# Attention feeding a two-layer MLP on one core: layer 2 of the third batch's last group in seven block products, and the attention of the last two chunks moved together

## The chip, the cores and the metric

One Trainium2 chip, one of its cores. The metric is the device time of one execution in microseconds (us), the median of several runs.

## What is computed

Two stages, in float32. Attention over 4 batches, 8 heads, 768 positions and a head size of 64: each query sees the keys within 16 positions and 24 summaries of 32 keys each (maximum of the keys, mean of the values). Its output, 3072 rows of 512, goes through a two-layer MLP.

```python
def _attn_ref(q, k, v):
    ...
    k_sum = k.reshape(B, H, nb, block, D).max(axis=3)
    v_sum = v.reshape(B, H, nb, block, D).mean(axis=3)
    scores_l = scale * np.matmul(q, k.transpose(0, 1, 3, 2))          # kept where |i - j| < 16
    scores_s = scale * np.einsum('bhsd,bhnd->bhsn', q, k_sum) + np.log(block)
    ...                                                               # softmax over both together
    return np.matmul(a, v_all)

def _moe_ref(x, w_in, w_out):      # x 3072 x 512, w_in 512 x 2048, w_out 2048 x 512
    h = x @ w_in
    g = np.maximum(0.01 * h, h)
    return g @ w_out
```

## The kernel before, in words

**Precision.** Every MLP operand is kept as two parts, hi and lo, and a product of two operands is three TensorE (PE) matmuls: hi by hi, lo by hi, hi by lo. A part is made by ScalarE (ACT; the hi part, a rounded copy) and VectorE (DVE; the lo part, the difference), so each new operand costs one instruction on each of the two.

**Stages.** The work runs in batches 0 to 3 of 768 rows, each of two chunks of 384. Batch 0 uses the plain product in both layers (`mlp`, lines 724 and 743 to 745). Batches 1 to 3 (`strassen`) take layer 1 as seven block products in place of eight, in Strassen's manner. The 16 feature tiles of 128 are taken in groups of four (n = 0 to 3), two pairs j of tiles in each. For a pair, the seven products (line 1090, names "1" to "7" in the order 1, 6, 7, 5, 2, 4, 3) go to four PSUM buffers, X (1, 2), Y (6), W (7, 4) and Z (5, 3). VectorE combines them (`add`, line 1126: U2, U3, P1), ScalarE and VectorE apply the activation and split the result (lines 1138 to 1152). Each product needs one half of the batch's input, made by `convert` (sums of the four quarters, line 955; their parts, lines 963 and 964), and a sum of weights, loaded from HBM into a ring of slots (line 1108).

**Layer 2, two ways.** In batches 1 and 2 a group's layer 2 is the plain one: six blocks of output (two halves h, three row tiles i), each of 12 matmuls of 512 columns (line 1229, tiles named L), and VectorE adds each finished block to the output row tile (line 1251, names y and rows). In batch 3 it is `second`: seven block products for each of three row tiles, each of 6 matmuls of 256 columns (line 1040, tiles named B2 or B, in the order 1, 4, 5, 7, 6, 2, 3). Its operands are G, the four activated quarters and the three differences and sums of them (`total`, line 1170, with parts at 1173 and 1177), and sums of output weights, made once for each pair j by `prepare2` (lines 865 to 877) and loaded again at line 1022. VectorE adds each product to its part of the output (`flush`, lines 1049 to 1053), named U, D, C21, C11 and C12; when the last group's product "6" is there, `merge` (line 1014) adds U into C21 and C12 and C21 into D. Two products share each PSUM half-buffer (4 and 7 in W, 5 and 3 in Z), so the later one waits until VectorE has read the earlier.

**Order.** `Plan.order` lays out the instructions of all engines by a list schedule: each operation has a due time (`prio`), and an engine takes the ready one that is due first. Due times come from a table and some numbers at the head of the file: `PLACE` for the attention of each chunk (in units of 1/24 of a batch's time), `P2` for `prepare2`, `PG` for the layer 1 weight sums, `CV` for the conversion of batch 1, `AHEAD` for how early weights are loaded. The attention of chunks 2 to 7 is spread in bursts between the MLP's matmuls (scores at line 371, transposes at 388, values at 394). Each engine then runs its list in order, and waits where an operand is not there yet.

**Buffers.** `settle` deals out slots. The ring of batch 3, `ring3`, has six slots in the input weights' place and six in output weights that are no longer read; batches 1 and 2 have `ring`, eight slots. Temporaries of batch 3 (`tmp3`) have five buffers and six pieces of `big`.

The change and the prediction touch `second` (lines 990 to 1070), `strassen` (1072 to 1259), `convert` (933 to 977) and `prepare2` (860 to 880).

Of the kernel before, what the change touches and what calls it, by code (L numbers as in the profile page):

```python
# [13 lines left out]
ALU = mybir.AluOpType  # L14
# [10 lines left out]
TPC = 3  # L25
T = 128 * TPC
# [10 lines left out]
SPL = 10  # L37
FP = 4
PARTS = [(0, 0, SPL), (1, 0, NF), (0, SPL, NF), (2, 0, FP), (3, 0, FP)]
CV = 26.64187  # L40
PG = 2.38096
P2 = 56.037475
XB = (0, 1, 1, 0)
SB = 2
PLACE = {0: (0.0, 1.0), 1: (13.07, 0.61), 2: (24.128751, 0.979249), 3: (33.570341, 0.464868), 4: (39.468202, 0.605071), 5: (53.449962, 0.361478), 6: (58.988368, 0.872963), 7: (67.160878, 1.199752)}
PLACE.update({c: (59.84 + UPC * (c - 6), 1.0) for c in range(8, NCH)})
LATE = 23.650498
RS = 8
GF = 4
L1W = 0.327846  # L50
AHEAD = 2.529455
BACC = {"dynamic_dma_scratch_size": 1024}

PL = -1.175
# [5 lines left out]
KP = -1.757  # L60
KS = -4
XW = 1
B1 = 2.589473
B2 = 2.761653
USQ = 1.589009
WT = 1.15
W0 = -1.523
WO = 1.029
# [95 lines left out]
def DVE(n, fast=False):  # L164
    return 65 + (0.52 if fast else 1.042) * n
# [6 lines left out]
def build(tc, ctx, a):  # L172
# [816 lines left out]

    def second(b, n, tn, g_op, done, rows):  # L990
        js, last = (2 * n, 2 * n + 1), n == NF // GF - 1
        letter = {"1": "X", "2": "X", "4": "W", "7": "W", "5": "Z", "3": "Z", "6": "Y"}
        goal = {"1": "U", "6": "U", "4": "D", "5": "D", "7": "C21", "2": "C11", "3": "C12"}
        part = {"D": (0, 256), "C21": (0, 0), "C11": (1, 0), "C12": (1, 256)}
# [8 lines left out]
        def keys(name, i):  # L1003
            return ("U", b, i) if name == "U" else ("y", b, part[name][0], i)
# [7 lines left out]

        def merge(x, y, i, t, after):
            return P.op("DVE", DVE(256), t, lambda: nc.vector.tensor_tensor(out=acc(x, i), in0=acc(x, i), in1=acc(y, i), op=ALU.add), after=after, use=[keys(x, i), keys(y, i)])

        for pos, q in enumerate(ORDER2):
            t = tn + L1W + pos * (6 - L1W) / 7
# [6 lines left out]
            for i in range(TPC):  # L1024
                tag, x = HALF2[s][i]
                kb = ("B2", b, n, tag)
                fresh = kb not in opened

                def block(q=q, i=i, tag=tag, x=x, kb=kb, fresh=fresh):
                    o = bank(kb, tag) if fresh else tl[kb]  # L1030
                    m = 0
                    for j in js:
                        gh, gl = (y[:, 128 * i:128 * i + 128] for y in g_of2(j, q))
                        if q in MEM2:
                            w = [ring(("r2", b, j, q))[:, l] for l in range(2)]
# [10 lines left out]
                def flush(name=name, q=q, i=i, kb=kb, x=x):  # L1046
                    y, z = acc(name, i), tl[kb][:, x:x + 256]
                    if n == 0 and q in "1723":
                        nc.scalar.copy(y, z)
                    elif n == 0 and q == "4":  # L1050
# [5 lines left out]
                e = ("ACT", ACT(256, True)) if n == 0 and q in "1723" else ("DVE", DVE(256))  # L1056
                p = P.op(e[0], e[1], t + 0.01 * i - 1.0, flush, after=[o] + done.get((name, i), []), use=[kb] + ([] if al else [k]), alloc=al)
                half[s, i] = [o, p]
                done[name, i] = [p]
                if not last:  # L1060
                    continue
                if q == "6":
                    for y in ("C21", "C12"):
                        done[y, i] = [merge(y, "U", i, t + 0.01 * i - 0.9, done[y, i] + [p])]
                    done["D", i] = [merge("D", "C21", i, t + 0.01 * i - 0.85, done["D", i] + done["C21", i])]
                if q in "63":
                    h = int(q == "3")
                    ky = ("y", b, h, i)
                    P.op("SP", 550, t + 0.5, lambda c=CPB * b + h, i=i, ky=ky: nc.sync.dma_start(out=a["out"][c * T + 128 * i:c * T + 128 * i + 128, :], in_=tl[ky]),
                         after=done["C11", i] + [p] if h else done["D", i], use=[ky], size=128 * 2048)  # L1070

    def strassen(b, t0):
        done, two = {}, b == B - 1
        n0 = FP // GF if b == 1 else 0
        if b == 1:
            done = {(h, i): [spill_op[2 + h, i]] for h in range(2) for i in range(TPC)}
# [16 lines left out]
            return P.op("PE", 6 * (T / 2.4 + 14.5), t, run, after=after + conv_op[b, pos], use=[kr, kx] + ([] if start else [kb]), alloc=[(tag, kb, 1)] if start else [])  # L1093

        for n in range(n0, NF // GF):
            tn = t0 + 6 * n
            g_op = {}
            for j in (2 * n, 2 * n + 1):
                K = lambda s, j=j: (s, b, j)
# [5 lines left out]
                for pos, q in enumerate(ORDER):  # L1105
# [6 lines left out]
                    p_op[q] = o = product(j, q, kr, kx, tags[s], (K(s), start), t, [lr] + hold.get(s, []), [])  # L1112
                    d = t - 1.0
                    def tmp(key):
                        if P.slot[key][0] != "q":
                            return new(P.slot[key], key, [128, T], bufs=1)
                        n = int(P.slot[key][1:])
                        tl[key] = raw[:, T * n:T * n + T]
                        return tl[key]
                    pool3 = "tmp3" if two else "tmp"  # L1120
                    ps = lambda s, K=K: tl[K(s)][:, :T]

                    def add(out, s, y, first, prio, after, K=K, ps=ps):
# [163 lines left out]
        t += UPC * (f1 - f0) / NF  # L1287
    for j in range(NF // 2):
        prepare(j, LEAD + 13 + PG * j)
        prepare2(j, LEAD + P2 + 3.5 * j)  # L1290
    for b in range(1, B):
        convert(b, LEAD + (24 * b - 3.2 if b > 1 else CV))
        strassen(b, LEAD + 24 * b)
# [1 line left out]
    P.settle("h", lambda t: ("h0", "h1"))  # L1295
    P.settle("big", lambda t: [f"big{n}" for n in range(BIG if t < LATE else 3)])
    P.settle("tmp", lambda t: ("gs", "ghi0", "glo0", "ghi1", "glo1"))
    P.settle("tmp3", lambda t: ["gs", "ghi0", "glo0", "ghi1", "glo1"] + [f"q{n}" for n in range(6)])
    P.settle("ring", lambda t: [f"r{n}" for n in range(RS)])
    P.settle("ring3", lambda t: [f"r{n}" for n in (0, 1, 2, 3, 6, 7)] + [f"b{n}" for n in range(6)])  # L1300
# [22 lines left out]
        begin(f"b{n}", region2[f] + region2[f + 2])  # L1323
    for i in range(TPC):
        begin(f"U{i}", early(0))
    for n in range(6):
        begin(f"q{n}", [o for p in {T * n // 512, (T * n + T - 1) // 512} for o in P.users["R", B - 1, p]])

# [68 lines left out]
```

## Time and profile before

| | |
|---|---|
| median of 3 runs | 613.03 us (612.43 to 613.39) |
| the profiled execution, its own time | 612.7 us |
| its span, first to last instruction | 610.9 us |
| TensorE busy | 604.9 us (99%), 4676 matmul records |
| VectorE busy | 469.7 us (77%) |
| ScalarE busy | 351.1 us (57%) |
| granted TensorE clock | 1.00 throughout |

A busy share counts the time in which at least one instruction of the engine is running. Matmuls overlap, so a busy TensorE is not yet one at its peak: the time of a stretch of matmuls is read from start to start. The groups of batches 2 and 3 lie at these times (us from the span's start): batch 2, last group, 453.13 to 485.94; batch 3, groups 0 to 3, from 485.94, 516.37, 546.51 and 576.65 to the end at 610.9.

### The profile page before, as it was taken

What the parts mean: (1) busy time and instruction counts of PE and PEld (TensorE: products, weight loads), DVE (VectorE), ACT (ScalarE), POOL (GpSimd) and SP (SyncE); (2) the same over time, 40 slices, a digit from 0 to 9 for tenths busy, and PEclk for the clock granted to TensorE, in tenths of its full rate; (3) what the DMA queues carried; (4) which work ended last, traced back from release to release, by engine and by line L of the source; (5) the groups of instructions that cost most, each with busy time, mean ns of one, the idle gap of its engine ahead of it and who ended that gap; (6) DMA issues with size and microseconds to landing.
All of it is one profiled execution on the core that took longest, in us unless ns stands there. A gap on an engine that the chain in (4) does not pass through costs nothing.

```text
span 610.9 us, 12895 instructions
## 1 busy us (share of the span) xinstructions
PE 604.9 (99%) x4676; PEld 540.1 (88%) x4676; DVE 469.7 (77%) x1281; ACT 351.1 (57%) x965; POOL 4.4 (1%) x10
## 2 busy tenths in 40 slices
PE   9999999999999999999999999999999999999997
PEld 6688889889888889999898897989889899999996
DVE  5899999953989995536688875877987783868687
ACT  5899996553776676416466665753717262606060
POOL 0200000000000000000000000000000000000000
PEclk9999999999999999999999999999999999999999
DMA  8898998896878826526497563866757484757552
GB/s 298 245 282 273 288 301 245 269 325 198 288 240 244 252 64 197 167 65 190 120 292 229 175 219 120 280 202 216 257 183 231 143 236 143 237 152 229 156 155 103
DMA packets 82926, 129.99 MB, mean 213 GB/s; under 512 B 7024, under 2 KB 50608, under 8 KB 82864
## 3 DMA queue, kind: packets, MB, share of 16 engines
q1 hardware_dynamic: 82864, 129.18, 68.1%
q8 instruction: 37, 0.61, 0.4%
q14 instruction: 25, 0.20, 0.1%
HBM read 97.72 MB, written 29.36 MB: 208 GB/s over the span
## 4 chain that ended last, share of the span: by engine, by line
PE 91%; DVE 4%; ACT 2%; DMA 1%; issue 0%; SPq 0%; DVEq 0%
PE L L1229 19%; PE h L724 12%; PE X L1090 8%; PE W L1090 8%; PE Z L1090 7%; PE B_a L1040 5%; PE a L744 4%; PE a L745 4%; PE a L743 4%; PE Y L1090 4%; PE B_s L1040 2%; PE B_to L1040 1%; ACT e L383 1%; PE vps L284 1%; DMA big<-in_k_dram 1%; DVE big L687 1%
## 5 line engine op out<-in xcount | busy, mean ns | idle before, releaser
L724 PE MATMUL h<-x,win_hi 128*128 128x384 f32 x320 | 82.7, 339 | 0.0
L383 ACT ACTIVATE e<-e,m 128x120 f32<-128x120 f32 x192 | 73.7, 388 | 3.7 <-DVE m L376 3.5
L1229 PE MATMUL L<-wout_hi,win_hi 128*128 128x512 f32 x168 | 66.5, 396 | 0.0
L1229 PE MATMUL L<-wout_hi,win_lo 128*128 128x512 f32 x168 | 65.7, 391 | 0.0
L1229 PE MATMUL L<-wout_lo,win_hi 128*128 128x512 f32 x168 | 65.6, 391 | 0.0
L724 PEld LDWEIGHTS h<-x,win_hi 128*128 128x128 f32 x320 | 57.6, 188 | 2.3 <-issue 0.2
L724 PE MATMUL h<-x,win_lo 128*128 128x384 f32 x160 | 53.8, 336 | 0.0
L743 PE MATMUL a<-wout_hi,ghi 128*128 128x512 f32 x120 | 48.4, 403 | 0.0
L745 PE MATMUL a<-wout_hi,glo 128*128 128x512 f32 x120 | 47.3, 394 | 0.0
L744 PE MATMUL a<-wout_lo,ghi 128*128 128x512 f32 x120 | 47.1, 392 | 0.1
L1229 PEld LDWEIGHTS L<-wout_hi,win_lo 128*128 128x128 f32 x168 | 31.5, 188 | 6.8
L383 ACT ACTIVATION_READ_ACCUMULATOR e<-e,m 128x1 f32 x192 | 36.7, 191 | 0.0
L1229 PEld LDWEIGHTS L<-wout_lo,win_hi 128*128 128x128 f32 x168 | 31.6, 188 | 5.7
L1229 PEld LDWEIGHTS L<-wout_hi,win_hi 128*128 128x128 f32 x168 | 31.6, 188 | 5.7
L734 DVE TENSOR_TENSOR glo<-gs,ghi 128x384 fp32r<-128x384 f32 x40 | 22.1, 554 | 17.0 <-ACT gs L728 16.3
L731 ACT ACTIVATE ghi<-h 128x384 fp32r<-128x384 f32 x40 | 19.6, 490 | 25.9 <-PE h L724 25.9
L1186 ACT COPY P<-X 128x384 f32<-128x384 f32 x19 | 9.0, 473 | 37.0 <-PE X L1090 36.9
L724 PEld LDWEIGHTS h<-x,win_lo 128*128 128x128 f32 x160 | 30.0, 188 | 0.0
L745 PEld LDWEIGHTS a<-wout_hi,glo 128*128 128x128 f32 x120 | 22.5, 188 | 5.4 <-DVE glo L734 0.4
L315 ACT COPY k<-big 128x288 f32<-128x288 f32 x64 | 24.8, 434 | 4.1 <-DMA big<-in_k_dram 4.0
L744 PEld LDWEIGHTS a<-wout_lo,ghi 128*128 128x128 f32 x120 | 22.6, 188 | 3.9 <-DVE wout_lo L693 0.4
L743 PEld LDWEIGHTS a<-wout_hi,ghi 128*128 128x128 f32 x120 | 22.6, 188 | 3.3
(620 smaller groups left out, 1625.9 us busy)
## 6 DMA issues: line engine op xcount, KB each, us to landing
win_hi<-sums SPq DMA_DIRECT2D x73, 256.0 KB
win_lo<-sums SPq DMA_DIRECT2D x71, 256.0 KB
big<-in_w_dram SPq DMA_DIRECT2D x32, 512.0 KB
sums<-big SPq DMA_DIRECT2D x32, 512.0 KB
v<-in_v_dram SPq DMA_DIRECT2D x32, 288.0 KB
big<-in_k_dram SPq DMA_DIRECT2D x16, 400.0 KB
k<-in_q_dram SPq DMA_DIRECT2D x32, 192.0 KB
wout_hi<-sums SPq DMA_DIRECT2D x21, 256.0 KB
```

The lines of the kernel that those rows point to most:

```text
L315: nc.scalar.copy(k, x)
L383: nc.scalar.activation(out=e[:, n], in_=e[:, n], func=AF.Exp, scale=-1.0, bias=m[:, n:n + 1], accum_out=z[:, n:n + 1])
L724: nc.tensor.matmul(h[:, :T], w[:, 512 * f + 128 * k:512 * f + 128 * k + 128], x[:, T * k:T * k + T], start=n == 0, stop=n == 11)
L731: nc.scalar.activation(out=gnew(tag, G("ghi", f)), in_=tl[G("h", f)][:, :T], func=AF.Prelu, alpha=0.01)
L734: nc.vector.tensor_tensor(out=gnew(tag, G("glo", f)), in0=tl[G("gs", f)], in1=tl[G("ghi", f)].bitcast(F32), op=ALU.subtract)
L743: nc.tensor.matmul(o, gh, wout_hi[:, f], start=f == f0, stop=False)
L744: nc.tensor.matmul(o, gh, wout_lo[:, f], start=False, stop=False)
L745: nc.tensor.matmul(o, gl, wout_hi[:, f], start=False, stop=f == f1 - 1)
L1040: nc.tensor.matmul(o[:, x:x + 256], g, w[l], start=fresh and m == 0, stop=m == 5, skip_group_check=True)
L1090: nc.tensor.matmul(o[:, :T], w[:, l, 128 * k:128 * k + 128], x[y][:, T * k:T * k + T], start=start and n == 0, stop=n == 5, skip_group_che ...
L1186: nc.scalar.copy(tmp(K("P1")), ps("X"))
L1229: nc.tensor.matmul(o, g, w[:, f], start=s + m == 0, stop=s == 1 and m == 5)
```

## The change

In batch 2 the last group (n = 3, feature tiles 12 to 15) takes its layer 2 from `second` as well. Since the output of batch 2 holds plain sums by then, `second` opens with one subtraction for each row tile (D becomes D - C21), product "1" starts U afresh by a ScalarE copy, and the merges end the batch. The group takes its loads from `ring3` and its temporaries from a new list, `tmp2`, with five pieces of `big` that K and V loads and `prepare2` used until then. The pairs 6 and 7 come first in `prepare2`. The table and the numbers of the order are new: the attention of chunks 2 to 7 has other places (chunk 5 starts at 47.91 in place of 53.45, chunk 7 takes 0.88 units for a tile in place of 1.20), and layer 1 has some 0.40 units in a group where it had 0.33.

```diff
-P2 = 56.037475
+N2 = 3
+P2 = 52.764603
-PLACE = {... 5: (53.449962, 0.361478), 6: (58.988368, 0.872963), 7: (67.160878, 1.199752)}
+PLACE = {... 5: (47.912053, 0.177619), 6: (59.244554, 0.831721), 7: (69.466097, 0.878535)}
-L1W = 0.327846
-AHEAD = 2.529455
+L1W = 0.399817
+AHEAD = 2.650579
...
     def second(b, n, tn, g_op, done, rows):
+        joins = b < B - 1 and n == N2
+        opens = b == B - 1 and n == 0
...
+        if joins:
+            for i in range(TPC):
+                rows.update(("y", b, h, i) for h in range(2))
+                for name in part:
+                    done[name, i] = done[part[name][0], i]
+                done["D", i] = done["C21", i] = [P.op("DVE", DVE(256), tn + 0.1 * i, lambda i=i: nc.vector.tensor_tensor(out=acc("D", i), in0=acc("D", i), in1=acc("C21", i), op=ALU.subtract),
+                                                      after=done["D", i], use=[keys("D", i)])]
...
+                copies = opens and q in "1723" or joins and q == "1"
...
-        done, two = {}, b == B - 1
+        done = {}
...
-            tn = t0 + 6 * n
+            tn, two = t0 + 6 * n, b == B - 1 or b == B - 2 and n >= N2
...
-                    pool3 = "tmp3" if two else "tmp"
+                    pool3 = ("tmp3" if b == B - 1 else "tmp2") if two else "tmp"
...
-        prepare2(j, LEAD + P2 + 3.5 * j)
+        prepare2(j, LEAD + P2 + 3.5 * ((j - 2 * N2) % (NF // 2)))
...
+    P.settle("tmp2", lambda t: ["gs", "ghi0", "glo0", "ghi1", "glo1"] + [f"m{n}" for n in range(5)])
...
+    for n in range(5):
+        begin(f"m{n}", early(1) + early(2))
```

**How the instructions move, on VectorE**, between the end of batch 2 and the first sums of batch 3 (line 1251 adds a plain block, 1066 is the flush of `second`, 1017 its merge, 955/956 and 964/965 are the conversion of batch 3's input, U2 and U3 the first sums of batch 3). Before:

```order
L964 TENSOR_TENSOR x0_80<-big_87,x0_80 128x768
L1251 TENSOR_TENSOR y_2_0_2_4688<-L_2_3_0_2_5775,y_2_0_2_4688 128x512
L955 TENSOR_TENSOR big_87<-big_87 128x768
L1251 TENSOR_TENSOR rows_3243<-L_2_3_1_0_5786,rows_3243 128x512
L964 TENSOR_TENSOR win_lo_74<-big_87,win_hi_73 128x768 x2
L1251 TENSOR_TENSOR rows_3243<-L_2_3_1_1_5812,rows_3243 128x512
L1251 TENSOR_TENSOR rows_3243<-L_2_3_1_2_5823,rows_3243 128x512
L1126 TENSOR_TENSOR U2_3_0_5873<-Y_3_0_5856,P1_3_0_5863 128x384
```

And now:

```order
L1066 TENSOR_TENSOR rows_3243<-rows_3243,B2_2_3_to_5747 128x256 x2
L1066 TENSOR_TENSOR rows_3243<-rows_3243,B2_2_3_s0_5757 128x256
L965 TENSOR_TENSOR win_lo_74<-big_87,win_hi_73 128x768
L965 TENSOR_TENSOR x3_86<-big_87,x1_82 128x768
L956 TENSOR_TENSOR big_87<-big_87 128x768
L1066 TENSOR_TENSOR rows_3243<-rows_3243,B2_2_3_a1_5808 128x256
L956 TENSOR_TENSOR big_87<-big_87 128x768
L1066 TENSOR_TENSOR rows_3243<-rows_3243,B2_2_3_a1_5808 128x256
L1066 TENSOR_TENSOR rows_3243<-rows_3243,B2_2_3_a2_5790 128x256
L965 TENSOR_TENSOR win_lo_74<-big_87,win_hi_73 128x768 x2
L965 TENSOR_TENSOR x0_80<-big_87,x0_80 128x768
L1139 TENSOR_TENSOR U2_3_0_6013<-Y_3_0_5953,P1_3_0_5961 128x384
```

Before, the conversion was over when the last blocks were added. Now seven of its eleven instructions stand among and behind the last flushes, and the three flushes of the last product (buffers a1 and a2) stand behind two of its sums.

**On TensorE**, the first products of batch 3 (the first matmul of each product is shown; X_3_0 is product buffer X of batch 3, pair 0, and W writes PSUM bank a1). Before:

```order
L1090 MATMUL X_3_0_5847<-x1_82,win_hi_73 128x384
...
L1090 MATMUL Y_3_0_5856<-win_hi_73 128x384
...
L1090 MATMUL W_3_0_5866<-win_hi_73,win_lo_74 128x384
...
L1090 MATMUL Z_3_0_5876<-win_hi_73,win_lo_74 128x384
...
L1090 MATMUL X_3_1_5915<-x1_82,wout_hi_75 128x384
```

And now:

```order
L1103 MATMUL X_3_0_5945<-x1_82,wout_lo_76 128x384
...
L1103 MATMUL Y_3_0_5953<-win_hi_73,wout_lo_76 128x384
...
L1103 MATMUL X_3_0_5945<-x1_82,win_lo_74 128x384
...
L1103 MATMUL W_3_0_5984<-win_hi_73 128x384
...
L1103 MATMUL X_3_1_5994<-x1_82,win_lo_74 128x384
...
L1103 MATMUL Z_3_0_6003<-win_hi_73 128x384
```

Product "2" of pair 0 (the second X) now stands ahead of the first W, and product "1" of pair 1 ahead of the first Z.

## Rows read from the trace of the kernel before

**Rows 1.** The page's head: the span, and of each engine the busy time, its share and the instructions.

```profile
span 610.9 us, 12895 instructions
PE 604.9 (99%) x4676; PEld 540.1 (88%) x4676; DVE 469.7 (77%) x1281; ACT 351.1 (57%) x965; POOL 4.4 (1%) x10
```

**Rows 2.** Busy time by stretch: a busy stretch of batches 1 and 2, the last two groups of batch 2, and the four groups of batch 3. Columns: stretch, its length, busy us of PE, PEld (weight loads), DVE, ACT and POOL with the instructions, granted clock, share of the DMA engines, GB/s.

```profile
303.03:344.94 41.91, 41.91 (x379) 36.71 (x379) 35.02 (x96) 27.38 (x80) 0.00 (x0) 1.00 0.78 233
417.44:453.13 35.69, 35.69 (x235) 31.79 (x235) 30.70 (x69) 17.44 (x41) 0.00 (x0) 1.00 0.70 239
453.13:485.94 32.81, 32.81 (x193) 29.49 (x193) 25.68 (x40) 16.35 (x28) 0.00 (x0) 1.00 0.54 171
485.94:516.37 30.43, 29.95 (x212) 29.73 (x211) 19.63 (x42) 14.19 (x35) 0.00 (x0) 1.00 0.72 214
516.37:546.51 30.14, 30.14 (x212) 29.75 (x211) 22.66 (x52) 11.28 (x25) 0.00 (x0) 1.00 0.63 193
546.51:576.65 30.14, 30.14 (x211) 29.76 (x211) 23.12 (x54) 10.91 (x24) 0.00 (x0) 1.00 0.62 193
576.65:610.90 34.25, 30.16 (x210) 29.56 (x209) 26.26 (x64) 10.91 (x24) 0.00 (x0) 1.00 0.38 123
```

**Rows 3.** The chain of work that ended last, in order of time: start us, length us, engine, tile, line, instructions. A whole plain group (72), one product of layer 1 (6), a burst of attention values, a run of 36 matmuls of `second`.

```profile
252.13 16.36 PE L L1229 x72
...
471.00 1.08 PE s_('B', 24)_5734 L394 x32
...
485.94 1.06 PE X L1090 x6
487.00 1.06 PE Y L1090 x6
...
533.25 4.30 PE B_a L1040 x36
```

**Rows 4.** TensorE's timeline where layer 2 begins in group 1 of batch 3: start us, length, line, operation.

```profile
529.93 1.03 PE L1090 MATMUL Z<-x,wout_lo 128*128 128x384 f32 x5
530.79 0.28 PE L1040 MATMUL B_to<-wout_hi,win_hi 128*128 128x256 f32 x1
```

**Rows 5.** All waits of TensorE over 0.2 us from 230 us on, and its weight loads' from 440 us on: us in total, times, longest.

```profile
PE B_a L1040 <- DVE y L1051: 0.5, 1, 0.5
...
PEld B_a L1040 <- DVE y L1051: 0.7, 1, 0.7
PEld B_s L1040 <- DVE big L1053: 0.5, 3, 0.2
```

**Rows 6.** VectorE's timeline where it is never idle: two additions of 512 and a pair of 768 (batch 2), the sums of 384 (batch 3, last group), and flushes and merges of 256. The pace is the distance of the starts.

```profile
475.18 0.68 DVE L1251 TENSOR_TENSOR y<-L,y 128x512 f32<-128x512 f32 x1
475.78 1.82 DVE L964 TENSOR_TENSOR win_lo<-big,win_hi 128x768 fp32r<-128x768 f32 x2
477.51 0.95 DVE L955 TENSOR_TENSOR big<-big 128x768 f32<-128x768 f32 x1
...
584.72 0.55 DVE L1170 TENSOR_TENSOR S<-big 128x384 f32<-128x384 f32 x1
585.30 0.56 DVE L1170 TENSOR_TENSOR big<-big,C 128x384 f32<-128x384 f32 x1
585.89 0.56 DVE L1170 TENSOR_TENSOR big<-big 128x384 f32<-128x384 f32 x1
...
586.84 0.55 DVE L1177 TENSOR_TENSOR win_lo<-big,win_hi 128x384 fp32r<-128x384 f32 x1
587.30 0.55 DVE L1126 TENSOR_TENSOR U<-W,U 128x384 f32<-128x384 f32 x1
587.77 0.55 DVE L1177 TENSOR_TENSOR win_lo<-S,win_hi 128x384 fp32r<-128x384 f32 x1
...
601.69 0.42 DVE L1014 TENSOR_TENSOR rows<-rows,big 128x256 f32<-128x256 f32 x1
602.03 0.41 DVE L1053 TENSOR_TENSOR big<-big,B_s 128x256 f32<-128x256 f32 x1
602.36 0.42 DVE L1014 TENSOR_TENSOR y<-y 128x256 f32<-128x256 f32 x1
```

**Rows 7.** VectorE's timeline from batch 2 to batch 3; in brackets the idle time before, and what ended it.

```profile
481.32 1.82 DVE L964 TENSOR_TENSOR win_lo<-big,win_hi 128x768 fp32r<-128x768 f32 x2
484.62 0.69 DVE L1251 TENSOR_TENSOR rows<-L,rows 128x512 f32<-128x512 f32 x1 [1.49 <-PE L L1229]
485.98 0.69 DVE L1251 TENSOR_TENSOR rows<-L,rows 128x512 f32<-128x512 f32 x1 [0.67 <-PE L L1229]
488.17 0.56 DVE L1126 TENSOR_TENSOR U<-Y,P 128x384 f32<-128x384 f32 x1 [1.50 <-PE Y L1090]
```

**Rows 8.** ScalarE's casts of 768 and 384 from 440 us on: busy us, mean ns, idle before.

```profile
L1173 ACT CAST win_hi<-big 128x384 fp32r<-128x384 f32 x9 | 4.4, 511 | 0.0
L963 ACT CAST win_hi<-big 128x768 fp32r<-128x768 f32 x4 | 3.3, 835 | 4.7 <-DVE big L955 4.7
```

More of the change, by code (lines that the diff above doesn't have):

```diff
@@ L39 @@
 PARTS = [(0, 0, SPL), (1, 0, NF), (0, SPL, NF), (2, 0, FP), (3, 0, FP)]
-CV = 26.64187
-PG = 2.38096
-P2 = 56.037475
+N2 = 3
+CV = 27.697487
+PG = 1.958344
+P2 = 52.764603
 XB = (0, 1, 1, 0)
 SB = 2
-PLACE = {0: (0.0, 1.0), 1: (13.07, 0.61), 2: (24.128751, 0.979249), 3: (33.570341, 0.464868), 4: (39.468202, 0.605071), 5: (53.449962, 0.361478), 6: (58.988368, 0.872963), 7: (67.160878, 1.199752)}
+PLACE = {0: (0.0, 1.0), 1: (13.07, 0.61), 2: (24.128751, 0.975826), 3: (33.609766, 0.479768), 4: (40.098663, 0.520481), 5: (47.912053, 0.177619), 6: (59.244554, 0.831721), 7: (69.466097, 0.878535)}
 PLACE.update({c: (59.84 + UPC * (c - 6), 1.0) for c in range(8, NCH)})
@@ L62 @@
 XW = 1
-B1 = 2.589473
-B2 = 2.761653
-USQ = 1.589009
+B1 = 2.648168
+B2 = 2.651731
+USQ = 0.165218
 WT = 1.15
@@ L1044, in second, with flush @@
                 opened.setdefault(kb, [o])
-                def flush(name=name, q=q, i=i, kb=kb, x=x):
+                copies = opens and q in "1723" or joins and q == "1"
+                def flush(name=name, q=q, i=i, kb=kb, x=x, copies=copies):
                     y, z = acc(name, i), tl[kb][:, x:x + 256]
-                    if n == 0 and q in "1723":
+                    if copies:
                         nc.scalar.copy(y, z)
-                    elif n == 0 and q == "4":
+                    elif opens and q == "4":
                         nc.vector.tensor_scalar(out=y, in0=z, scalar1=-1.0, scalar2=None, op0=ALU.mult)
@@ L1055, in second @@
                 k = keys(name, i)
-                e = ("ACT", ACT(256, True)) if n == 0 and q in "1723" else ("DVE", DVE(256))
+                e = ("ACT", ACT(256, True)) if copies else ("DVE", DVE(256))
                 p = P.op(e[0], e[1], t + 0.01 * i - 1.0, flush, after=[o] + done.get((name, i), []), use=[kb] + ([] if al else [k]), alloc=al)
@@ L1114, in tmp @@
                     def tmp(key):
-                        if P.slot[key][0] != "q":
+                        if P.slot[key][0] not in "qm":
                             return new(P.slot[key], key, [128, T], bufs=1)
-                        n = int(P.slot[key][1:])
-                        tl[key] = raw[:, T * n:T * n + T]
+                        x = T * int(P.slot[key][1:]) + (3072 if P.slot[key][0] == "q" else 1024)
+                        tl[key] = big[:, x:x + T]
                         return tl[key]
-                    pool3 = "tmp3" if two else "tmp"
+                    pool3 = ("tmp3" if b == B - 1 else "tmp2") if two else "tmp"
                     ps = lambda s, K=K: tl[K(s)][:, :T]
```

## The prediction, made before the run

> **What bounds the kernel now.** I read the page's head first: TensorE is busy in 604.9 of 610.9 us [rows 1]. A busy TensorE may still stand in a wait, so I looked at its waits next: from 230 us on there is one over 0.2 us, in the first group of batch 3, 0.5 us before a product whose half-buffer VectorE had not yet read [rows 5]. The clock is 1.00 in every stretch, and VectorE and ScalarE have idle time in each of them [rows 2]. So TensorE's own matmuls set the time where the change lies. What is worth something is fewer or shorter matmuls, as long as the other engines still hand over their operands in time. The chain gives the price of a stretch of matmuls: here its pieces are TensorE's, one behind the other [rows 3].
>
> **Part 1, the matmuls exchanged.** The group loses 72 matmuls of 512 columns and gets 7 x 3 x 6 = 126 of 256. The 72 took 16.36 us [rows 3], 0.227 each. 36 of the others took 4.30 us [rows 3], 0.119 each, so 126 take 15.05 with no wait among them: **-1.3 us**. Layer 1 keeps its 84 matmuls: in group 1 of batch 3 they start with the group at 516.37 [rows 2], and layer 2 begins at 530.79 [rows 4], so 14.4 us. That group needs 30.14 us in all [rows 2], which leaves 15.7 for its layer 2: 0.7 us of it waits, among them those of [rows 5]. I count such waits in part 2, from 15.05.
>
> **Part 2, the work on VectorE.** Between its first sum of the group and its first sum of batch 3, VectorE had 18 instructions of 384 columns, 11 of 768 (the conversion), 6 of 512, and one each of 1024 and 256. Now it has 32 of 384, 11 of 768 and 27 of 256 (18 flushes, 9 merges). Back to back they start 0.47 (384), 0.33 (256), 0.87 (768) and 0.60 us (512) apart [rows 6]. Before: 8.4 + 9.5 + 3.6 + some 1.5 = 23 us, in a group of 32.8 [rows 2], and it stood idle 1.5, 0.7 and 1.5 us around the group's end [rows 7]. Now: 14.9 + 9.5 + 9.0 = 33.4 us, in a group where TensorE needs 14.4 + 15.05 and 1.3 for one burst of attention values (1.08 [rows 3] with its ends), 30.8 us. VectorE has more work than the group lasts, and it falls behind.
>
> Whom does that hold up? In the last group of batch 3 VectorE's first difference (tile S) starts at 584.72, 8.1 us after the group's start at 576.65 [rows 2, 6], with the same seven instructions ahead of it. From there I go by the new order: up to the flush that releases PSUM bank a1 stand 25 instructions of 384, 8 of 768 and 26 of 256, so 11.7 + 6.9 + 8.7 = 27.3 us. Three waits add some 0.75: two differences that need the one before start 0.58 apart, not 0.47 [rows 6], 0.1 each; a cast for gx has to stand behind two casts of 768 on ScalarE, 0.84 each [rows 8], some 0.4; the last W product 0.1. The flush is then over 36.2 us after the group's start, and seen by TensorE a little later, 36.3. TensorE is done with the group at 30.8 and can do X, Y and X of batch 3 meanwhile, 1.04 each [rows 3], so it stands at W at 33.9. The product W writes a1 and must wait: **+2.4 us** of waits up to here, those inside layer 2 among them. Its bounds: 0, if the order lets VectorE start its dense stretch earlier than the pattern of batch 3 (where it starts 8.1 us after the group), and 3.4, if the casts on ScalarE cost another microsecond.
>
> Queued behind W on TensorE are all other products. Behind the late flush on VectorE stand three more instructions of the conversion and the first sums of batch 3, so product Z ("5"), which reads one of these, can wait again for 0.3 us, and the second pair's W for 0.5.
>
> **Part 3, the first group of batch 3.** It took 30.43 us [rows 2], of which 14.4 + 15.05 are matmuls: 1.0 us of waits. The new order runs both X products of a pair early, and layer 2 begins between the last products of layer 1, with two blocks of product "2" ahead of "5", so that the wait on the half-buffer [rows 5] should go. Against that stand the two waits after W. I take 0.4 in place of 1.0, **-0.6 us**; bounds -1.0 and +0.3.
>
> **At nothing.** The attention makes the same matmuls, in as many bursts after 233 us (21 entries from other matmuls in either order), so its place costs TensorE nothing; its work on VectorE and ScalarE falls into groups with idle time: 30.70 of 35.69 us busy in the group before, and no wait of TensorE even where VectorE had 35.02 of 41.91 [rows 2, 5]. `prepare2`, all of it ahead of the group now, is covered by the same. If that cover were gone, its last two or three pairs would come on top of part 2. The three subtractions that open `second` lie in the group before, 1 us of VectorE's idle time. ScalarE gets 9 instructions more in all and was busy for 16.35 of 32.81 us [rows 2]. SP's queue carries eight more loads of 256 KB: 171 GB/s become some 240, and 239 and 233 ran without a wait of TensorE [rows 2, 5]. The six stores of batch 2 now wait on SP for the merges and the last flushes. Twelve of the 14 loads for the next layer 1 stand ahead of them; behind are two for products that TensorE reaches over 12 us later, and the loads of the next layer 2.
>
> **A rule weighed.** The rows show VectorE instructions of 0.55 us that start 0.47 us apart: the next starts before the last has ended [rows 6]. The Trainium skill (VectorE: DVE Perf Modes, The DRAIN you can't avoid) says that the next instruction does not start until the pipeline has emptied. Its own later section grants that one which isn't held starts earlier, and the trace here sides with that. By whole durations, part 2's stretch would be 25 x 0.55 + 8 x 0.95 + 26 x 0.42 = 32.3 us, 5.0 more.
>
> **The sum.** -1.3 + 2.4 - 0.6 = +0.5 us. Against the profiled execution's own 612.7 us (span 610.9) that is 613.2; the median of the runs is 0.3 above that execution, so **613.5 us** for the median. 0.2%, or 1.2 us, is about what a measurement of this kernel can tell from no change, so the forecast is: no difference.
>
> **The rivals.**
> - *VectorE keeps up.* Were its dense stretch to start 2 us earlier, W's bank would be free when TensorE gets there. For it: in the group as it was, VectorE stood idle for 3.7 us at the end [rows 7], and conversion work can fill gaps. Against it: the first sums depend on products that come 1.04 us apart, so nothing can be drawn forward. Part 2 is then 0.5: -1.3 + 0.5 - 0.6 = -1.4 us, 611.6. Chance 0.22.
> - *VectorE is late by more, and the first group of batch 3 gains nothing* (the other side). The place is the end of batch 2: the conversion's halves go back and forth between VectorE and ScalarE, 0.84 a cast [rows 8], and W, Z and the next W wait one after another. Part 2 at 3.4 and part 3 at 0: +2.1 us, 615.1. It decides from the point where part 2 passes 3.1, for then the sum passes +1.2. For it: the order itself takes products out of turn here. Against it: batch 3's groups, with 22 to 23 us of VectorE work, hardly wait [rows 2, 5]. Chance 0.20.
> - *VectorE's instructions don't overlap.* Then part 2 is 5 us larger: some 618.5. All of [rows 6] speaks against it here. Chance 0.02. This is the rule named above.
> - *The loads come late.* The group draws on the ring of 12 slots, six of them in output weights that the plain groups were still reading, and eight loads more have to pass. If one load holds up TensorE for 2 us, 615.5. Against it: the same ring with the same loads feeds batch 3, at 193 to 214 GB/s, with no wait for a load in [rows 5]. Chance 0.04.
>
> **How the numbers follow.** The forecast, no difference, has the remaining 0.52. Faster is the first rival, 0.22; slower are the other three, 0.26. The range goes from 611.5 (the first rival's time) to 615.1 (the second's); what lies beyond is the lower tail of the first, the upper tail of the second, and most of the last two, under 0.2 together.
>
> **What the profile after would show.** Part 1 is right if 126 matmuls stand in the group, 0.119 us apart, and its layer 2 spans 15.1 to 15.7 us. Part 2 is right if VectorE is never idle for long from 8 us after the group's start until past its end, and TensorE waits for a flush (line 1066) or a part of the conversion (line 965) between the first X and the first Z of batch 3, 1.5 to 3 us in all; wrong if TensorE runs through there, or if ScalarE or a load ends the wait. Part 3 is right if the group from the first X of batch 3, less the waits of part 2, takes under 30 us, and groups 1 to 3 take what they took. The prediction as a whole is wrong if time changes before the last group of batch 2, where I left the moved attention at nothing.

## The result and the profile after

The change takes 619.56 us (median of 4 runs, 619.35 to 620.37) where the kernel before takes 613.21 (612.43 to 613.61): a ratio of 1.0108, 95% interval 1.0095 to 1.0120. It is slower by 1.1%. A second set of runs (e16_change2 below) has 619.0 and 1.0102 (1.0089 to 1.0115). The prediction had no difference, and 615.1 as its upper end.

The page's head, to be read against [rows 1]: 54 more matmuls, VectorE 11.4 us busier, the span 7.6 us longer.

```profile
span 618.5 us, 13081 instructions
PE 607.0 (98%) x4730; PEld 542.1 (88%) x4730; DVE 481.1 (78%) x1319; ACT 351.5 (57%) x974; POOL 4.4 (1%) x10
```

Where the time went is read from the first layer-1 product of each group (us, profiled executions; the last column is a second profile of the change). The starts are the first matmul's own; those of before lie 0.16 us ahead of the starts in [rows 2], which are the chain's and stand where the matmul in front has ended.

| stretch | before | change | again |
|---|---|---|---|
| start to group 1 of batch 1 | 233.59 | 234.74 | 233.49 |
| from there to the last group of batch 2 | 219.38 | 219.43 | 218.96 |
| last group of batch 2 | 32.81 | 34.13 | 34.12 |
| first group of batch 3 | 30.43 | 32.50 | 32.51 |
| groups 1, 2, 3 of batch 3 | 30.14, 30.14, 30.04 | 30.96, 30.95, 30.84 | 30.96, 30.96, 30.85 |
| from the last matmul's start | 4.40 | 4.94 | 4.57 |

The 1.15 us at the start are not in every execution of the change: its second has them not. From the last group of batch 2 to the last matmul everything repeats within 0.02 us. The same stretches by busy time (columns as in [rows 2]): the clock is 1.00 in each, TensorE now has idle time in each, and groups 1 to 3 are longer although VectorE is no busier in them.

```profile
454.17:488.30 34.13, 33.09 (x249) 31.89 (x248) 28.02 (x62) 15.58 (x33) 0.00 (x0) 1.00 0.69 217
488.30:520.80 32.50, 30.64 (x213) 29.63 (x211) 26.17 (x53) 15.96 (x37) 0.00 (x0) 1.00 0.69 221
520.80:551.76 30.96, 30.28 (x213) 29.77 (x211) 22.41 (x52) 11.42 (x26) 0.00 (x0) 1.00 0.61 190
551.76:582.71 30.95, 30.26 (x212) 29.76 (x211) 23.02 (x54) 10.91 (x24) 0.00 (x0) 1.00 0.62 187
```

TensorE's waits from 230 us on, against the single one of [rows 5]: ten in place of one, four of them on a bank `s1` (VectorE's read of it, the flush at line 1066, writes `big`), one of 1.3 at product W.

```profile
PE B_s L1051 <- DVE big L1066: 1.7, 4, 0.4
PE B_a L1051 <- DVE y L1066: 1.3, 4, 0.5
PE W L1103 <- DVE rows L1066: 1.3, 1, 1.3
PE B_a L1051 <- DVE y L1064: 0.5, 1, 0.5
```

**The batch boundary.** TensorE's timeline (idle time in brackets) and VectorE's at the first W product. TensorE has done X, Y and X and is ready at 491.4. W writes bank a1; VectorE reads that bank in the additions to `rows` at 491.20 and 492.40. VectorE was last idle at 479 and 481, 0.87 and 0.33 us, for blocks that TensorE had not finished. From then on nine closing additions (line 1017) and five of the conversion's instructions (lines 956, 965) stand ahead of the read at 492.40, with no gap between any two: VectorE is behind, as [rows 7] with its idle 1.5, 0.7 and 1.5 us was not.

```profile
490.38 1.24 PE L1103 MATMUL X<-x,win_lo 128*128 128x384 f32 x6
492.88 0.44 PE L1103 MATMUL W<-win_hi 128*128 128x384 f32 x1 [1.26 <-DVE rows L1066]
```

```profile
479.19 1.08 DVE L1066 TENSOR_TENSOR y<-y,B_a 128x256 f32<-128x256 f32 x3 [0.87 <-PE B_a L1051]
...
481.40 1.42 DVE L1066 TENSOR_TENSOR y<-y,B_a 128x256 f32<-128x256 f32 x4 [0.33 <-PE B_a L1051]
...
484.59 0.42 DVE L1017 TENSOR_TENSOR y<-y,big 128x256 f32<-128x256 f32 x1
...
486.60 1.10 DVE L1017 TENSOR_TENSOR y<-y 128x256 f32<-128x256 f32 x3
...
488.60 0.96 DVE L965 TENSOR_TENSOR win_lo<-big,win_hi 128x768 fp32r<-128x768 f32 x1
489.47 0.96 DVE L965 TENSOR_TENSOR x<-big,x 128x768 fp32r<-128x768 f32 x1
490.33 0.96 DVE L956 TENSOR_TENSOR big<-big 128x768 f32<-128x768 f32 x1
491.20 0.42 DVE L1066 TENSOR_TENSOR rows<-rows,B_a 128x256 f32<-128x256 f32 x1
491.54 0.96 DVE L956 TENSOR_TENSOR big<-big 128x768 f32<-128x768 f32 x1
492.40 0.76 DVE L1066 TENSOR_TENSOR rows<-rows,B_a 128x256 f32<-128x256 f32 x2
```

**Groups 1 to 3.** TensorE's timeline in group 1 of batch 3 of the change. The block of product "7" in bank a0 comes right after the last of "5" and waits 0.27 for a flush; the second block in bank s1 comes right after the first and waits 0.41, until VectorE has read the first.

```profile
541.63 0.51 PE L1051 MATMUL B_a<-win_hi,gx 128*128 128x256 f32 x3
542.42 0.50 PE L1051 MATMUL B_a<-win_lo,win_hi 128*128 128x256 f32 x2 [0.27 <-DVE y L1066]
...
545.73 0.52 PE L1051 MATMUL B_s<-win_lo,gx 128*128 128x256 f32 x3
546.66 0.51 PE L1051 MATMUL B_s<-win_hi 128*128 128x256 f32 x2 [0.41 <-DVE big L1066]
```

A bank holds two half-buffers, and the program makes a block wait for the read of either half: the second s1 block writes a half that nothing had used in this group. The plan that sets the order knows only of the own half (`half`), so it puts such blocks side by side without seeing a price. The Trainium skill (PSUM — Partial Sum Buffer, PSUM bank collisions raise a hardware error) wants semaphores by bank (more finely, by bank and 32 partitions), not by address; the waits in this trace do go by bank.

### The profile page after: what moved, and what is told of

It is laid out like the page before. It is cut to its first block, busy times and chain, and to the rows that moved or that the text cites. A ratio compares the mean times of both kernels' runs of the same rounds, so it can differ in the third digit from the quotient of the medians.

```text
span 618.5 us, 13081 instructions
## 1 busy us (share of the span) xinstructions
PE 607.0 (98%) x4730; PEld 542.1 (88%) x4730; DVE 481.1 (78%) x1319; ACT 351.5 (57%) x974; POOL 4.4 (1%) x10
## 4 chain that ended last, share of the span: by engine, by line
PE 77%; DVE 14%; ACT 4%; DMA 3%; issue 2%; DVEq 0%; ACTq 0%
PE L L1242 16%; PE h L725 12%; PE W L1103 5%; PE X L1103 5%; PE Z L1103 5%; PE a L745 4%; PE a L746 4%; PE a L744 4%; PE B_a L1051 4%; PE Y L1103 3%; DMA big<-in_w_dram 2%; PE spare L1359 2%; ACT e L384 2%; DVE U L1139 1%; DVE y L1066 1%
## 5 line engine op out<-in xcount | busy, mean ns | idle before, releaser
L1242 PE MATMUL L<-wout_hi,win_hi 128*128 128x512 f32 x144 | 57.9, 402 | 0.1
L1242 PE MATMUL L<-wout_hi,win_lo 128*128 128x512 f32 x144 | 56.3, 391 | 0.0
L1242 PE MATMUL L<-wout_lo,win_hi 128*128 128x512 f32 x144 | 56.2, 391 | 0.0
L1242 PEld LDWEIGHTS L<-wout_hi,win_lo 128*128 128x128 f32 x144 | 27.0, 188 | 5.9
L1242 PEld LDWEIGHTS L<-wout_hi,win_hi 128*128 128x128 f32 x144 | 27.1, 188 | 5.6 <-DVE y L1264 0.5
L1242 PEld LDWEIGHTS L<-wout_lo,win_hi 128*128 128x128 f32 x144 | 27.1, 188 | 4.7
```

Source lines behind the costliest of these rows:

```text
L1242: nc.tensor.matmul(o, g, w[:, f], start=s + m == 0, stop=s == 1 and m == 5)
```

## The experiments

Each kernel is timed beside the kernel before on the same chip (medians of that: 613.05 to 613.34 us). First comes its own median in us, then its ratio to the kernel before with the 95% interval. "Group" times are distances of first layer-1 products, as above.

**e1_blocks and e2_blocks_only: the order of the blocks.** `L1W` is the time that the plan gives to layer 1; the change raised it. Here it is set for groups 1 to 3 of batch 3 alone, in the change to the old value, in the kernel before to the new one (the same lines, values exchanged):

```
+LW = lambda b, n: 0.327846 if b == B - 1 and n > 0 else 0.399817
-            t = tn + L1W + pos * (6 - L1W) / 7
+            t = tn + LW(b, n) + pos * (6 - LW(b, n)) / 7
...
```

> The change, with the time that the plan gives to layer 1 put back to the old 0.327846 in groups 1 to 3 of batch 3 alone; that puts the first s1 block of the sixth product ahead of the seventh's a0 blocks again, as in the kernel before, and moves nothing else. If the order of these blocks makes the wait (a block waits for VectorE's read of its own PSUM bank), each of the three groups loses its two waits of 0.4 and 0.6 us and goes from 30.95 to 30.15: 617.2 in all, 2.4 below the change. If VectorE is simply late in batch 3, the waits move to other blocks and the time stays at 619.5 (0.3 less at most).

> The kernel before, with only the new 0.399817 in groups 1 to 3 of batch 3: no seven-product layer 2 is added and no attention moved. If the block order makes the wait, these three groups go from 30.15 to 30.95 and the time to 615.6 (2.4 above 613.2). If the waits of the change came from its load on VectorE, which this kernel lacks, the time is 613.2 and at most 0.3 above.

e1: 616.53, ratio 1.0058 (1.0035 to 1.0080); e2: 615.97, ratio 1.0043 (1.0027 to 1.0060). Group 1, 2, 3: 30.15, 30.14, 30.02 in e1, 30.94, 30.95, 30.84 in e2. The order makes the 0.8 us, in both directions, with or without the change; VectorE's load has no part in it. One number in the plan's table did this, and the first s1 block moved past the two a0 blocks. In e1's timeline it stands between "5" and "7", and of both waits less than 0.1 us is left:

```profile
539.81 0.52 PE L1052 MATMUL B_a<-win_hi,gx 128*128 128x256 f32 x3
540.17 0.40 PE L1052 MATMUL B_s<-win_hi 128*128 128x256 f32 x2
...
540.88 0.40 PE L1052 MATMUL B_a<-win_lo,win_hi 128*128 128x256 f32 x2
...
543.31 0.50 PE L1052 MATMUL B_s<-win_hi 128*128 128x256 f32 x2
```

**e3_loads: the start.**

```
-B1 = 2.648168
+B1 = 2.589473
```

> The change, with the plan's old start of the key and value loads of batch 1 (B1 2.589473); the transfers of the start then stand in the order of the kernel before. If the changed order (a load of values of batch 1 ahead of a weight load) made the 1.15 us that the change was late at the first group, that goes: first layer-1 product of batch 1 at 233.6 and 618.4 in all. If it was the spread of one execution, it is 619.5, and the first group stands anywhere between 233.6 and 234.8 in both.

618.67, ratio 1.0094 (1.0064 to 1.0123), and group 1 of batch 1 at 234.09; with the new order e1_blocks has 233.74. So the new order of the loads can start as early as the old one, and executions differ there by as much as 1.15 us. Whether the change makes late starts more frequent is open: the eleven profiles with `second` in batch 2 start at 233.5 to 236.1, six of them at 234.7 or later, the seven without it at 233.6 to 234.1.

**e4_bank and e11_swap: the W wait, by order.** e4 draws the flushes of the last product, "3", ahead of the conversion (they are three, not the six of the expectation below); e11 exchanges the joined group's last two products.

```
-                p = P.op(e[0], e[1], t + 0.01 * i - 1.0, flush, ...
+                p = P.op(e[0], e[1], t + 0.01 * i - (1.0 + 3 * (joins and q in '3')), flush, ...
```

```
-        for pos, q in enumerate(ORDER2):
+        order2 = ORDER2[:5] + ("3", "2") if joins else ORDER2
+        for pos, q in enumerate(order2):
```

> The change, with the six additions of the joined group's last product three units earlier in VectorE's order, so that they stand ahead of the conversion's instructions. If bank a1, released late, is what the first W product of batch 3 waits for, the wait of 1.4 us goes and the time is 618.1; half of it, 618.8, if conversions that now come later hold products 2, 4 or 3 in their turn. If VectorE is the limit of that stage whatever the order, the wait turns up at another product and the time is 619.5.

> The change, with the last two products of the joined group exchanged (the third before the second), so that banks a1 and a2 are written and read 2.2 us sooner; no work is taken away. If the late release of bank a1 alone makes the wait, it goes and the time is 618.1. If VectorE has no time left in that stage, a conversion's instruction comes later by as much, and an operand takes the bank's place, as at product 3 (Z) and product 1 of the second half in e4_bank and e7_gpsimd: 619.0 to 620.

e4: 620.26, ratio 1.0117 (1.0087 to 1.0147), first group of batch 3 33.35. e11: 619.69, ratio 1.0103 (1.0088 to 1.0118), 32.66. Neither gains. TensorE's waits from 230 us on, of e4 and then of e11: W's wait on the bank is gone in both, and product X waits for ScalarE's copy of its bank instead, 1.2 and 1.5.

```profile
...
PE X L1103 <- ACT C L1154: 1.2, 1, 1.2
...
PE W L1103 <- DVE win_lo L965: 0.4, 1, 0.4
```

```profile
PE X L1104 <- ACT C L1155: 1.5, 1, 1.5
```

ScalarE was late because of VectorE: in e11 its cast of 768 columns stands ahead of that copy and waits for the conversion's difference, which VectorE reaches at 491.72.

```profile
492.70 0.83 ACT L964 CAST win_hi<-big 128x768 fp32r<-128x768 f32 x1 [0.36 <-DVE big L956]
493.44 0.48 ACT L1163 ACTIVATE win_hi<-X 128x384 fp32r<-128x384 f32 x1
493.82 0.48 ACT L1155 ACTIVATE C<-X 128x384 f32<-128x384 f32 x1
```

**e5_no_sums and e9_no_sums2: the W wait, by load.** The nine closing additions are left out, so that three quarters of batch 2's output lack a term; in e9 a row is also stored only after its last flush.

```
-                if q == "6":
+                if q == "6" and not joins:
...
-                         after=done["C11", i] + [p] if h else done["D", i], ...
+                         after=done["C11", i] + [p] if h else done["D", i] + done["C21", i], ...
```

> The change, without the nine closing additions (256 columns each) in the joined group, so that three quarters of the second batch's rows lack a term; 9 x 0.335 = 3.0 us less for VectorE in that stage, nothing else taken away. If VectorE's load is what makes the first W product of batch 3 wait, the 1.4 us go, the first group of batch 3 falls from 32.50 to 31.1 and the time to 618.1. If a chain of the conversion (its operands, its banks, ScalarE) is the limit, the group stays at 32.1 to 32.5 and the time at 619.2 or above.

> e5_no_sums with its stores mended: the nine closing additions of the joined group are left out again (three quarters of the second batch's rows lack a term), but a row is stored only after its last flush, so that no flush waits for a store as it did there. VectorE's load as the cause of the W wait: the joined group is at 34.1 as in the change, the first group of batch 3 at 30.4 as in e5_no_sums, and the time 617.4. If the W wait was gone in e5_no_sums only because the joined group before it took 1.1 us longer, the first group is back at 31.5 or above and the time at 618.5.

e5: 619.44, ratio 1.0089 (1.0062 to 1.0117), a miss by its time: without the additions a row was stored before its last flush, the flush waited for the store, and the joined group took 35.26; the group after it fell to 30.39. e9: 616.85, ratio 1.0057 (1.0041 to 1.0073), in e9's rows the joined group as in the change and the next one at 30.36, with no wait at W. So 3.0 us less work on VectorE give back 2.1; moving the work about, in e4 and e11, gave nothing.

```profile
452.41:486.53 34.12, 33.09 (x249) 31.88 (x248) 27.92 (x56) 16.42 (x34) 0.00 (x0) 1.00 0.75 233
486.53:516.89 30.36, 30.17 (x212) 29.75 (x211) 23.29 (x49) 15.21 (x36) 0.00 (x0) 1.00 0.70 220
```

**e7_gpsimd: the work on another engine.** e4's edit, the old `L1W` in all of batch 3, the old `B1`, and:

```
-            return P.op("DVE", DVE(256), t, lambda: nc.vector.tensor_tensor(...
+            e, w = ("POOL", nc.gpsimd) if joins else ("DVE", nc.vector)
+            return P.op(e, ..., t, lambda: w.tensor_tensor(...
```

> The change, with the old layer-1 time in the whole of batch 3 (block order of before), batch 1's loads of before, the nine closing additions of the joined group on GpSimd in place of VectorE, and that group's last six additions earlier. The block order gives back 2.4, the W wait 1.4: 615.6. If GpSimd takes over 1 us for one addition, the last additions of the joined group (which need its sums) hold bank a1 and the W wait stays: 617.0. To be below the 613.2 of before it would have to lose the 1.5 us of waits in the joined group too, which nothing here removes.

617.05, ratio 1.0057 (1.0038 to 1.0076): the second case by its time, not by its place. The first group of batch 3 takes 33.22; W waits only 0.2 us for its bank, and Z 1.7 us for the conversion. GpSimd's and VectorE's timelines say why: an addition takes GpSimd 0.7 to 1.45 us, and beside it VectorE's instructions of 768 columns with both inputs in SBUF last 1.52 in place of 0.95 [rows 6]. Those with one input in PSUM keep 0.41.

```profile
484.89 1.45 POOL L1019 TENSOR_TENSOR y<-y 128x256 f32<-128x256 f32 x1
486.30 2.15 POOL L1019 TENSOR_TENSOR y<-y,big 128x256 f32<-128x256 f32 x2
```

```profile
486.33 1.52 DVE L957 TENSOR_TENSOR big<-big 128x768 f32<-128x768 f32 x1
487.77 0.41 DVE L1068 TENSOR_TENSOR rows<-rows,B_s 128x256 f32<-128x256 f32 x1
488.11 0.41 DVE L1068 TENSOR_TENSOR rows<-rows,B_a 128x256 f32<-128x256 f32 x1
488.44 1.53 DVE L957 TENSOR_TENSOR big<-big 128x768 f32<-128x768 f32 x1
```

**e6_attention_only and e14_attention2: the moved attention.** The constants `CV`, `PG`, `P2`, `PLACE`, `AHEAD` and `B2` of the change in a kernel that keeps the plain layer 2 in batch 2 and the old `L1W` and `B1`. So it is the place of the attention together with that of the conversion of batch 1, the prepared sums and the loads:

```
-N2 = 3
+N2 = 4
-L1W = 0.399817
+L1W = 0.327846
```

> The kernel before with the change's times for attention, for the conversion and for layer 2's prepared sums, and its own for layer 1 (0.327846) and for batch 1's loads; layer 2 of the last group of batch 2 stays as it was. It has the moved attention alone. If the moved attention is covered, as the prediction had it: 613.2, within 0.4. If it makes the 1.1 us of waits that the change has more between its first layer-1 product of batch 1 and the last group of batch 2: 614.3.

> The kernel of e6_attention_only once more, with more rounds. A cost of the moved attention: 614.5 and a ratio to the kernel before of 1.001 to 1.003, without 1.000 in its interval. No cost: 613.3 to 613.6, and first-group start and waits that differ from e6_attention_only's own execution.

e6: 614.53, ratio 1.0004 (0.9986 to 1.0022), which settles nothing; e14: 614.79, ratio 1.0032 (1.0021 to 1.0043). These constants cost. Start distances of TensorE's matmuls beyond their pace (0.120, 0.1735 and 0.227 us for 256, 384 and 512 columns) sum to 4.45 us before, from group 1 of batch 1 to 455 us; here to 5.50 and 5.28, in the change's two profiles to 5.49 and 5.05. All four kernels with the old place (before, e2, e8, e15) have 4.45. One place is a product X in e6, where ScalarE has run eight exponentials of the moved attention (from 283.98 on) ahead of the copy that frees X's bank; ScalarE's timeline and TensorE's:

```profile
286.93 0.19 ACT L384 ACTIVATION_READ_ACCUMULATOR e<-e,m 128x1 f32 x1
287.02 0.47 ACT L1154 ACTIVATE C<-X 128x384 f32<-128x384 f32 x1
```

```profile
287.55 1.14 PE L1103 MATMUL X<-x,win_lo 128*128 128x384 f32 x5 [0.18 <-ACT C L1154]
```

What ScalarE is late for, and why the size differs from one execution to the next, stands in VectorE's timeline. Its maximum over the keys of batch 3's second pair of heads (`ksum`) came 76 us after the first product of group 1 of batch 1 in the kernel before and comes 47 us after it in the new order, and now VectorE waits there for the load of these keys (1.8 us in e6); its sum P and ScalarE's exponentials queue behind. In e1, in the change and in e4:

```profile
281.07 0.95 DVE L250 TENSOR_REDUCE ksum<-big 128x24 f32<-128x768 f32 x1 [1.90 <-DMA big<-in_k_dram]
```

```profile
282.92 0.95 DVE L249 TENSOR_REDUCE ksum<-big 128x24 f32<-128x768 f32 x1 [2.74 <-DMA big<-in_k_dram]
```

```profile
285.52 0.95 DVE L249 TENSOR_REDUCE ksum<-big 128x24 f32<-128x768 f32 x1 [4.05 <-DMA big<-in_k_dram]
```

Over the kernels with the change's order there, the sum above follows this wait: 4.7 for waits of 1.5 to 1.9 us (e1, e3, e9, e12), 4.9 for 2.2 (e7), 5.05 for 2.3 (e16), 5.35 for 2.7 (e5), 5.5 for 2.7 (the change), 5.6 for 2.9 (e11), 6.7 for 4.05 (e4). The kernels with the old place have no such wait. So this order costs 0.3 us in each of these executions, and up to 2.0 more where the keys land later. No run puts the load of the keys back alone.

**e8_bank_rule and e15_bank_rule2: the plan told of the bank.** In the kernel before:

```
-            ... half.get((s, i), []) + opened.get(kb, []),
+            ... half.get((s, i), []) + (read.get(kb, []) or opened.get(kb, [])),
...
                 half[s, i] = [o, p]
+                read[kb] = [p]
```

> The kernel before, with one wait added to its plan: a block of layer 2 comes after the last VectorE read of its PSUM bank, whichever half that read. The plan then spreads blocks of one bank apart in all four groups of batch 3. If the wait for a read of the same bank is what is left there (0.45 us in each of groups 1 to 3, 0.74 in the first), the four groups lose 0.3 each: 612.0. If the new order makes as many waits of another kind (operands g, loads), 613.2 to 614.5.

> The kernel of e8_bank_rule once more, beside e13_bank_attention on the same chip: 611.2, ratio 0.996 to 0.997, whatever the moved attention costs.

611.25, ratio 0.9962 (0.9950 to 0.9975), and 610.93, ratio 0.9971 (0.9959 to 0.9983): faster than both kernels. Batch 3 takes 123.02 us in place of 125.1 (from the first matmul's own start; the last four rows of [rows 2], from the chain's, have 124.96), with the same matmuls.

```profile
485.84:608.86 123.02, 119.42 (x841) 118.58 (x839) 92.76 (x210) 47.37 (x108) 0.00 (x0) 1.00 0.58 182
```

**e10_change_bank_rule, e12_all_plan, e13_bank_attention: with the rule, what is the change worth?** e10 is the change with the rule and the old `L1W`; e12 the change with the rule, the old `L1W` in batch 3 and e11's exchange; e13 is e15 with the moved attention of e14.

> The change, with the old layer-1 time 0.327846 everywhere and the added wait of e8_bank_rule in the plan (a block of layer 2 after the last VectorE read of its bank). 619.5 - 2.4 for the blocks of groups 1 to 3, 1.8 for what e8_bank_rule gained beside that in batch 3, 1.2 for the two waits of the joined group on a flush and on a bank: 614.1, with the W wait still there. If VectorE's backlog at the joined group takes that 1.2 and more in another place, 615.5 or above.

> The change, with the old layer-1 time in batch 3, the added bank wait in the plan, and the last two products of the joined group exchanged. By the sums of the last two: 614.1 with the W wait, 612.8 without it, so level with the kernel before (613.3) and above the 611.25 of e8_bank_rule, which has the bank rule without the change. Below 611.25 would say that the change itself is worth its 1.3 us once the plan knows the bank; above 614.5 that the joined group's VectorE load stays on the path whatever the order.

> e8_bank_rule with the moved attention of e6_attention_only: the same blocks in all four groups of batch 3 and no seven-product layer 2 in batch 2, so against e15_bank_rule2 only the place of the attention (with the conversion and the prepared sums) differs. If the moved attention costs what the medians of e6_attention_only showed, 612.4 here, 1.2 above the bank rule alone. If it costs nothing, 611.3, within 0.3.

e10: 616.07, ratio 1.0047 (1.0029 to 1.0066); its X and Z wait 1.4 and 0.9 us for the conversion. e12: 612.91, ratio 1.0004 (0.9992 to 1.0016). e13: 612.75, ratio 0.9998 (0.9990 to 1.0007), 1.8 above e15. Against the 611 of the rule alone the change as a whole still costs e12 1.7 to 2.0 us. Its profile beside e15's, by start distances beyond the matmuls' pace, says where: the first group of batch 3 has 2.7 us in e12 and none in e15 (TensorE's idle times there are Z 0.8 and 0.4 and X 0.3; start distances count more than the idle time at each), 0.3 lie before the joined group, and the matmuls give back 1.2. So what remains of VectorE's waits costs over twice what the exchange gives, even with the rule. The 1.8 us of e13 can't be taken off from that: with the old `L1W` in batches 1 and 2 as well, e13 has another order ahead of the joined group, and its profile loses 0.9 us there where e12's loses 0.3.

**e16_change2: the change once more.**

> The change itself once more. If its late start (1.15 us at the first group) belongs to the one execution that was profiled, the group starts at 233.6 to 234.2 here and the waits of the joined group and batch 3 are the same to 0.1 us; if it belongs to the kernel, 234.7 again. The time 619.5 either way, within 0.5.

619.00, and the column "again" above: the late start is not in this execution, and from the joined group to the last matmul the times are the same.

## Why the prediction was wrong, step by step

Against e16's span, 5.5 us over before's: -1.2 from the matmuls, +0.6 from waits before the last group of batch 2, +1.5 from waits in that group, +2.1 in the first group of batch 3, +2.4 in groups 1 to 3, +0.2 at the end, -0.1 at the start. This is the shortest of its four executions; by the medians the change costs 5.9 to 6.3. The first profile, 2.1 us longer, has the difference at the start (1.25), before the joined group (0.46) and at the end (0.36).

- **Part 1 was right.** The 126 matmuls stand 0.119 to 0.120 us apart; the price, -1.2 to -1.3, is what the stretch gives when its waits are taken off: 34.1 is about 30.8 + 2.0 of waits + 1.4 for six plain matmuls that the plan now draws into this group. The 14.4 us for a layer 1 are 0.16 too short, because the group's start was the chain's; the 84 matmuls take 14.57, and groups 1 to 3 of before had 0.45 us of waits each, not 0.7.
- **Part 2 had the right mechanism, and was too small.** The first W product of batch 3 waits for VectorE's read of bank a1, 1.3 us, behind the conversion; e9 shows that the load and not the order is the cause. I had let the waits inside the joined group count towards the 2.4, since TensorE would then reach W later. It did, but VectorE was later too: the read of a1 was over 38.7 us after the group's start, not 36.2. It began its dense stretch at 9.6 us, not 8.1, behind the six plain matmuls, which delay TensorE as much; and inside that stretch it stood idle for 1.2 us, waiting for TensorE's blocks, which the count of back-to-back instructions had at nothing. So both waits came: 1.5 in the group (0.3 for a copy of ScalarE, 0.7 and 0.6 for flushes, start distances beyond the pace) and 1.4 at W. 3.0 in place of 2.4, inside the bounds of 0 to 3.4.
- **Part 3 failed.** The first group was to lose 0.6 us of waits. Less W's wait it gained 0.6: the half-buffer wait stayed (0.64), for its block still comes right behind the last of "5", and a block of bank `to` now waits 0.28 for a copy of ScalarE. The two blocks of product "2" that were drawn forward bought nothing here.
- **"Groups 1 to 3 take what they took" is the step that cost most,** 2.4 of the 5.5. The difference of orders showed one s1 block on the other side of two a0 blocks in each of these groups, and I gave it no price, because no row showed a wait there and the plan's own dependencies had none. The wait that did stand in [rows 5] in the first group, and the three of weight loads on B_s, were its trace: blocks of one bank close together.
- **"At nothing": the moved attention is not free.** With the constants that go with it, it costs 1.7 us in e14. I had argued from idle shares (30.70 of 35.69 us) and from the same number of bursts, which is right (21 in either order); the cost lies in what the moved work waits for. VectorE waits 1.5 to 4.1 us for keys that it now needs 29 us sooner, and on ScalarE a copy that frees a bank stands behind that and behind 3 us of exponentials. In the change's two profiles this makes 1.0 and 0.6 us of waits of TensorE. Of e14's 1.7, the trace shows about 1.0, in pieces of up to 0.4; the profiled execution is the fastest of its six (614.0), so that the rest would lie in executions without a profile, which is not shown. The subtractions and prepared sums made no wait of TensorE over 0.2 us.
- **The rivals.** VectorE did not keep up. The weight loads that the fourth rival names were in time; the load that was late, of keys, is in none of the rivals. The second rival, VectorE later and nothing gained in the first group, is the nearest; its 615.1 lacks groups 1 to 3 and the attention. That VectorE's instructions don't overlap did not happen: 0.96 us ones start 0.87 apart above.

## What to carry to other kernels

When a planner's constants change, every move in the order has to be priced, also in stages that the change doesn't speak of, and by the resource that the program's waits go by (a PSUM bank), not by the one that the plan models (half of it). Work that is moved forward takes its loads along, and idle shares don't show whether these land in time. Where an engine was busy without a gap into a stage boundary, order did not help: in e4, e10, e11 and e12 the wait moved to another bank or operand, and the first group of batch 3 kept 2.7 to 3.7 us of waits (the change itself 2.8); with less work, in e9, it kept 0.7. The one other engine tried, GpSimd, left 3.5. A wait that the plan does not know of was cheap to remove: telling it gave 0.3 to 0.4% where the change lost 1%.

## What the runs showed of the hardware

GpSimd is no spare VectorE here: nine additions of 256 columns took it 9.7 us in all, where VectorE needs 3.0, and VectorE's instructions of 768 columns with both inputs in SBUF were stretched from 0.95 to 1.52 meanwhile. The Trainium skill (SBUF — State Buffer, Who interferes with whom) says that such instructions contend with GpSimd's reads; the trace agrees, and shows that those with one input in PSUM are spared.
